# One key load of an attention decode kernel cut by rows: the last sixteen partitions first, in five pieces, then the other 112

## The chip, the cores and the metric

The kernel runs on one core of a Trainium2 chip. The metric is the device time of one execution in microseconds (us). Three runs of the kernel before gave a median of 678.96 us, from 678.95 to 679.36. One further execution was profiled: it took 678.87 us, of which 677.6 us are the span that the profile shows.

## What is computed

One decoded token passes through an attention block and a gated feed-forward block, each behind an adaptive layer norm. The attention reads a key and a value cache of 32 heads, 16384 tokens and 128 numbers per head in bf16: two times 134 MB, which is nearly all that the kernel reads.

```python
mod = (silu(c) @ w_mod).reshape(1, 6, 1, 640)          # sa, ca, ga, sb, cb, gb
h = layernorm(x) * (1 + ca) + sa
q = (h @ wq).reshape(1, 1, 32, 128).transpose(0, 2, 1, 3)
scores = einsum('bhqd,bhkd->bhqk', q, k_cache) * 128 ** -0.5
o = einsum('bhqk,bhkd->bhqd', softmax(scores), v_cache)
x = x + ga * (o.reshape(1, 1, 4096) @ wo)
h = layernorm(x) * (1 + cb) + sb
x = x + gb * ((silu(h @ w_gate) * (h @ w_up)) @ w_down)
```

## The kernel before, in words

The heads are taken in 16 pairs (`NP = 16`). For one pair, the 128 partitions hold two heads by 64 stretches of tokens: partition r holds 256 consecutive tokens (`T2 = 256`) of 128 numbers, which is 65,536 bytes. The keys of a pair are thus one load of 8 MiB with 128 rows of 64 KiB, and so are its values. `k_src(p)` is that view of the key cache. The keys go into `kring`, which has two slots; pair p uses slot `p % 2`. The values go into `vbuf`, which has one slot (the last pair's values go into slot 0 of `kring`).

Per pair, the vector engine (DVE) multiplies the keys by the query in place and folds the 128 products of a token down to 16 columns. This is done in two halves c = 0 and 1: `mult` (L544), `fold` (L549), `foldb` (L554). The tensor engine (PE) adds the 16 columns into the scores (`R`, L534). For pair p-1 the largest score is found and the exponentials are taken while pair p is being multiplied (`largest`, `weigh`), and then PE multiplies them with the values (`pv`, L508). Pairs 0 and 15 go through `score_end` (L562, L568) instead.

All large loads are issued by SyncE (SP) in program order through one helper, `dma` (L90). Each waits on SP for the work that frees its buffer:

- `load_k(p)` for p of 2 and more waits for the last `R` of pair p-2 (`o_R[p - 2]`), which is the last reader of that slot.
- `load_v(p)` waits for `pv` of pair p-1 (`o_pv[p - 1]`).
- The order on SP is: the weights of the modulation and of q, keys 0 (in two halves by tokens, `KCUT`), keys 1, values 0, then in turn keys p+1 and values p, and at the end `wo`, the gate and up weights and five loads of the down weights.

Every load has its own counting semaphore by a key, here `("k", p % 2, c)`, where c numbers the loads of the pair. The first multiplication of pair p waits for `d_k[p][-1]`, the last load of its keys, which in the kernel before is the only one for all pairs from 1 on.

For PE the pairs 1 to 14 are one loop; for DVE and ScalarE the loop begins with pair 3 (`FIRST = 3`), and SP has no loop. Pair 2, the third one, is thus written out on DVE, and its extra waits are plain instructions there.

Of the kernel before, what the change touches and what calls it, by code (L numbers as in the profile page):

```python
# [37 lines left out]
class _Plan:  # L38
# [38 lines left out]
    def op(self, eng, fn, deps=(), name="", chan=None):  # L77
        o = _Op(eng, fn, list(deps), name, len(self.ops), self.loop.get(eng), chan)
        o.sig = chan is not None
        self.ops.append(o)  # L80
        return o

    def dma(self, out_ap, in_ap, key, deps=(), name="", eng="sp", noncontig=False):
        nc = self.nc

        def fn(e, out_ap=out_ap, in_ap=in_ap, noncontig=noncontig):
            if noncontig:
                with nc.allow_non_contiguous_dma(reason="tiny vector layout change"):
                    return e.dma_start(out_ap, in_ap)
            return e.dma_start(out_ap, in_ap)  # L90

        return self.op(eng, fn, deps, name, chan=self.dma_chan(key))
# [116 lines left out]
def build(nc, A_x, A_k, A_v, A_wq, A_wo, B_wg, B_wu, B_wd, c_in, w_mod, out):  # L209
# [6 lines left out]
    T2 = 2 * S // 128  # L216
# [16 lines left out]
    with es:  # L233
        plan = _Plan(nc, es)
        op, dma = plan.op, plan.dma
        POOL, ACT, DVE, PE = "pool", "act", "dve", "pe"

        def sb(name, shape, dtype):
            return es.enter_context(nc.sbuf_tensor(name, list(shape), dtype))

        kring = sb("kring", [128, 2, T2, 128], BF16)
# [27 lines left out]
        rows = qbc[0:1].rearrange("p a d -> p (a d)")[:, 0:2 * D].rearrange("p (j n) -> p j n", j=2)  # L269
# [67 lines left out]
        k_src = lambda p: A_k[0, 2 * p:2 * p + 2].rearrange("h (q t) d -> (h q) t d", q=64)  # L337
# [95 lines left out]
        def pick(half, n, o_m, free):  # L433
# [14 lines left out]
            deps=[o_m0, o_xn], name="t1")  # L448
# [9 lines left out]
        o_qev = []  # L458
        o_q = []
        for g in range(H // 4):  # L460
            b = g % 2
# [9 lines left out]
            for half in range(2):  # L471
# [4 lines left out]
                    deps=[o_q[g]], name="qbc%d_%d" % (g, half)))  # L476
# [4 lines left out]
        d_k, d_v = [None] * NP, [None] * NP  # L481
        o_R, o_pv, o_exp, o_nb, o_mx, o_acc, o_ot = ([None] * NP for _ in range(7))
        KCUT = [0, T2 // 2, T2]
        LCUT = [0, T2 // 2, 7 * T2 // 8, T2]
        VCUT = [0, T2]
        v_at = lambda p: vbuf[:] if p < NP - 1 else kring[:, 0]

        def load_k(p):
            deps = [o_R[p - 2]] if p >= 2 else ([o_mod[1]] if p == 1 else [])
            cuts = KCUT if p == 0 else [0, T2]  # L490
            d_k[p] = [dma(kring[:, p % 2, a:b], k_src(p)[:, a:b], ("k", p % 2, c), deps=deps, name="dma_k%d_%d" % (p, c))
                      for c, (a, b) in enumerate(zip(cuts, cuts[1:]))]

        def load_v(p):
            deps = [o_R[NP - 2]] if p == NP - 1 else [o_pv[p - 1]] if p >= 1 else [o_q[-1]]
# [43 lines left out]
        def score(p, c, between=None):  # L539

            kv4 = kring[:, p % 2].rearrange("p t (a d) -> p t a d", a=2)[:, :, :, QW * c:QW * c + QW]
            def f_mult(e):
                q4 = qbc[:, bass.ds(plan.at(p), 1), :].rearrange("p o (a d) -> p o a d", a=2)[:, :, :, QW * c:QW * c + QW].broadcast_to([128, T2, 2, QW])
                return e.tensor_tensor(out=kv4, in0=kv4, in1=q4, op=ALU.mult)  # L544
            o_m = op(DVE, f_mult,
                     deps=[d_k[p][-1]] + o_qev[p // 2], name="mult%d_%d" % (p, c))
            if between:
                between[0]()
            o_f = op(DVE, lambda e: e.tensor_tensor(out=kv4[:, :, 0], in0=kv4[:, :, 0], in1=kv4[:, :, 1], op=ALU.add),  # L549
                     deps=[o_m], name="fold%d_%d" % (p, c))  # L550
            if between:
                between[1]()
            lo = kv4[:, :, 0]
            return op(DVE, lambda e: e.tensor_tensor(out=lo[:, :, 0:QR], in0=lo[:, :, 0:QR], in1=lo[:, :, QR:QW], op=ALU.add),  # L554
                      deps=[o_f], name="fold%d_%db" % (p, c))

        def score_end(p, c, between=None):

            cut = KCUT if p == 0 else LCUT
            n = cut[c + 1] - cut[c]  # L560
            kv = kring[:, p % 2, cut[c]:cut[c + 1]]
            o = op(DVE, lambda e: e.tensor_tensor(  # L562
                out=kv, in0=kv, in1=qbc[:, p, :].unsqueeze(1).broadcast_to([128, n, 128]), op=ALU.mult),
                deps=[d_k[p][min(c, len(d_k[p]) - 1)]] + o_qev[p // 2], name="mult%d_%d" % (p, c))
            for i, w in enumerate((64, 32, 16)):
                if between and i < 2:
                    between[i]()
                o = op(DVE, lambda e, w=w: e.tensor_tensor(out=kv[:, :, 0:w], in0=kv[:, :, 0:w], in1=kv[:, :, w:2 * w], op=ALU.add),  # L568
                       deps=[o], name="fold%d_%d_%d" % (p, c, w))
            return o  # L570

        def reduce_end(p, a, b, fold):
            def f_R(e):
                last = None
                for d in range(16):
                    last = e.matmul(S_ps[:, a:b], lhsT=ident[:], rhs=kring[:, p % 2, a:b, d], start=(d == 0), stop=(d == 15))  # L576
                return last
            return op(PE, f_R, deps=[fold, o_ident, o_exp[p - 1] if p else o_gb], name="R%d_%d" % (p, a))

        def largest(p):  # L580
            o_pm = op(DVE, lambda e: e.tensor_reduce(  # L581
                out=pm[:, p % 2:p % 2 + 1], in_=S_ps[:, 0:T2], axis=AX.X, op=ALU.max), deps=[o_R[p]], name="pm%d" % p)
            o_d2 = op(ACT, lambda e: e.activation(out=d2[:], in_=negid[:], func=ACTF.Copy, scale=pm[:, p % 2:p % 2 + 1]),  # L583
                      deps=[o_pm, o_negid], name="d2_%d" % p)
            o_mx[p] = op(PE, lambda e: e.matmul(mx_ps[:, 0:64], lhsT=bd_f[:], rhs=d2[:], start=True, stop=True),  # L585
                         deps=[o_d2, o_bd1, o_bd2, o_nb[p - 1] if p >= 1 else o_m0], name="mx%d" % p)
# [14 lines left out]
        def step(p):  # L601
            reduce_mm(p, 0, score(p, 0, before(p)))
            pv(p - 1)
            o_R[p] = reduce_mm(p, 1, score(p, 1))
            diag(p - 1)

        load_k(0)
        load_k(1)
        load_v(0)
        score_end(0, 0)  # L610
        o_R[0] = reduce_end(0, 0, T2, score_end(0, 1))
        NLOOP = NP - 2
        for p in range(1, NP - 1):
            plan.in_loop(("pe",), "pairs", p - 1, NLOOP)
            if p >= FIRST:
                plan.in_loop(("act", "dve"), "pairs", (p - FIRST) // 2, (NP - 1 - FIRST) // 2)
            load_k(p + 1)
            step(p)
            load_v(p)
# [13 lines left out]
        for c in (1, 2):  # L633
            f1 = score_end(PL, c)
            o_R[PL] = reduce_end(PL, LCUT[c], LCUT[c + 1], f1)
        largest(PL)
# [9 lines left out]
        for i, (b, r0, r1) in enumerate(DOWN):  # L646
            if b is None:
                dst, src = wt_v, B_wd[NF * 128:F, :].rearrange("q (h n) -> (q h) n", h=2)
            else:
# [8 lines left out]
                 deps=[o_exp[PL], o_rz, o_onesf, o_rstd], name="L")  # L658
# [7 lines left out]
                  deps=[o_z, o_e32] + o_qev[-2], name="am")  # L666
# [21 lines left out]
        def f_cols(e):  # L688
# [14 lines left out]
            deps=[o_ga, o_xf], name="x1")  # L703
# [18 lines left out]
        def gate0(o_xc1):  # L722
# [6 lines left out]
            deps=[o_xc1, o_rstd1, o_onep_b], name="t2")  # L729
# [6 lines left out]
                  deps=[o_xsp, o_ot[PL], o_strips], name="x1_rows")  # L736
# [10 lines left out]
        for i, (b, r0, r1) in enumerate(DOWN):  # L747
# [14 lines left out]
            if i == 0:  # L762
                o_tw = op(PE, lambda e: e.matmul(attn_ps[:, 8:9], lhsT=twice[64:128].rearrange("p q h -> p (q h)"), rhs=gu_col[64:128, NF:FCH], start=True, stop=True),
                          deps=[o_gum, o_twice, o_abf], name="twice_gu")
                o_guh = op(DVE, lambda e: e.tensor_tensor(out=gu_half[:], in0=attn_ps[:, 8:9].broadcast_to([128, 2]), in1=even[:], op=ALU.mult),
                           deps=[o_tw, o_even], name="gu_half")
# [10 lines left out]
def bass_adaLN_cond__gqa_block_cached__swiglu_ffn__decode_kernel(  # L777
    nc: bass.Bass,
    A_x: bass.AP,
    A_k_cache: bass.AP,  # L780
    A_v_cache: bass.AP,
    A_wq: bass.AP,
    A_wo: bass.AP,
    B_x: bass.AP,
    B_w_gate: bass.AP,
    B_w_up: bass.AP,
    B_w_down: bass.AP,
    c: bass.AP,
    w_mod: bass.AP,
    out: bass.AP,  # L790
):
    build(nc, A_x, A_k_cache, A_v_cache, A_wq, A_wo, B_w_gate, B_w_up, B_w_down, c, w_mod, out)
# [28 lines left out]
```

## Time and profile before

| What | Value |
|---|---|
| Median of 3 runs | 678.96 us (678.95 to 679.36) |
| Profiled execution | 678.87 us, span 677.6 us |
| Bytes read from HBM | 290.47 MB |
| Busy share of the span | DVE 76%, PE 54%, ACT 7% |
| Mean transfer rate | 429 GB/s |
| Loads of keys | 17 issues, 16 pairs |

The span is what the table's shares refer to; the 1.3 us between span and execution lie around it. A busy share is a mean over stages, so the DMA rows by slices and the waits say more than it does about what sets the end. "DMA share" is the mean busy share of the core's 16 DMA engines; "SPq" rows are SP issuing a transfer, not the transfer itself.

### The profile page before, as it was taken

The numbers are of one execution on the slowest core, as the hardware profiler recorded it, in microseconds if no ns is written. First come the engines' busy times: TensorE is split into PE (matmuls) and PEld (weight loads), VectorE is DVE, ScalarE is ACT, GpSimd is POOL, SyncE is SP. The second block draws the span as 40 slices with busy tenths as digits, with TensorE's granted clock in tenths as the row PEclk, the third lists the DMA queues.
The fourth block names the chain that finished last, engine by engine and source line by source line (L and its number), as shares of the span: only waits on it lengthen the run. The fifth ranks groups of instructions, "written<-read, shape, count | busy, mean of one in ns | idle before, by whom it ended". The sixth has DMA issues, their size and how long they took to land.

```text
span 677.6 us, 5406 instructions
## 1 busy us (share of the span) xinstructions
PE 363.6 (54%) x2069; PEld 144.5 (21%) x2069; DVE 514.1 (76%) x190; ACT 46.4 (7%) x146; POOL 0.7 (0%) x6
## 2 busy tenths in 40 slices
PE   2420475755728284654818375562828465481776
PEld 1100122221212122221302122121212222130335
DVE  2189997959596896959597795959699695959912
ACT  1120000100000000000000010000000000000010
POOL 0000000000000000000000000000000000000000
PEclk9675565555757565565756556575656556565765
DMA  9999999999999999999999999999999999999997
GB/s 375 440 459 433 433 437 430 433 430 433 433 434 433 433 433 433 433 433 433 433 433 433 433 433 433 433 433 433 433 433 433 433 433 433 433 433 433 430 400 318
DMA packets 6355, 290.58 MB, mean 429 GB/s; under 512 B 714, under 2 KB 972, under 8 KB 1356
## 3 DMA queue, kind: packets, MB, share of 16 engines
q1 hardware_dynamic: 6340, 290.48, 99.3%
q8 instruction: 5, 0.08, 0.0%
q14 instruction: 2, 0.02, 0.0%
q10 hardware_dynamic: 8, 0.00, 0.0%
HBM read 290.47 MB, written 0.00 MB: 429 GB/s over the span
## 4 chain that ended last, share of the span: by engine, by line
DMA 49%; DVE 30%; issue 13%; PE 8%; SPq 0%; DVEq 0%
DMA kring<-in_A_k_cache_dram 45%; DVE kring L544 10%; PE psb L534 7%; DVE kring L549 6%; DVE kring L562 5%; DVE kring L568 5%; DMA kring<-in_B_w_down_dram 4%; DVE kring L554 3%; SPq L90 0%; DVE pm L581 0%; DVE nb L589 0%; PE psb L576 0%; PE psb L758 0%; DVEq L191 0%; DVEq L544 0%
## 5 line engine op out<-in xcount | busy, mean ns | idle before, releaser
L544 DVE TENSOR_TENSOR kring<-kring,qbc 128x16384 bf16<-128x16384 bf16 x28 | 243.3, 8690 | 96.1 <-DMA kring<-in_A_k_cache_dram 96.1
L534 PE MATMUL psb<-kring,ident 128*128 x448 | 197.5, 607 | 120.3 <-DVE kring L554 120.3
L549 DVE TENSOR_TENSOR kring<-kring 128x8192 bf16<-128x8192 bf16 x28 | 123.8, 4421 | 0.5
L534 PEld LDWEIGHTS psb<-kring,ident 128*128 128x128 bf16 x448 | 54.0, 120 | 248.0 <-issue 247.2
L508 PE MATMUL psb<-vbuf,PZ 128*8 128x512 bf16 x960 | 80.9, 511 | 0.0
L585 PE MATMUL psb<-d,bd_f 128*128 128x64 f32 x32 | 11.0, 446 | 118.5 <-ACT d L583 118.5
L554 DVE TENSOR_TENSOR kring<-kring 128x4096 bf16<-128x4096 bf16 x28 | 64.1, 2288 | 0.5
L562 DVE TENSOR_TENSOR kring<-kring,qbc 128x16384 bf16<-128x16384 bf16 (+2 forms) x5 | 34.9, 6981 | 23.4 <-DMA kring<-in_A_k_cache_dram 23.4
L508 PEld LDWEIGHTS psb<-vbuf,PZ 128*8 128x8 bf16 x960 | 26.6, 108 | 58.9 <-issue 49.0
L576 PE MATMUL psb<-kring,ident 128*128 128x256 bf16 (+3 forms) x64 | 14.5, 392 | 43.2 <-DVE kring L568 43.2
L585 PEld LDWEIGHTS psb<-d,bd_f 128*128 128x128 f32 x32 | 8.0, 312 | 120.7 <-DVE pm L581 111.3
L568 DVE TENSOR_TENSOR kring<-kring 128x2048 bf16<-128x2048 bf16 (+7 forms) x15 | 32.2, 2148 | 0.4
L523 PEld LDWEIGHTS psb<-sel,acc_sb 128*128 128x128 f32 x128 | 28.5, 311 | 7.7 <-issue 4.3
L523 PE MATMUL psb<-sel,acc_sb 128*128 128x2 f32 x128 | 25.6, 322 | 1.1 <-ACT acc_sb L514 1.1
L514 ACT ACTIVATE acc_sb<-psb 128x512 f32<-128x512 f32 x16 | 9.6, 598 | 210.7 <-PE psb L508 210.7
L593 ACT ACTIVATE PZ<-psb,nb 64x256 bf16<-64x256 f32 x32 | 15.0, 469 | 64.8 <-DVE nb L589 64.6
L576 PEld LDWEIGHTS psb<-kring,ident 128*128 128x128 bf16 x64 | 6.4, 121 | 50.5 <-DVE kring L568 44.3
L583 ACT ACTIVATE d<-negid,pm 128x64 f32<-128x64 f32 x16 | 5.6, 348 | 153.2 <-DVE pm L581 153.2
L466 PE MATMUL psb<-vbuf,h_col 128*128 128x512 bf16 x40 | 10.9, 443 | 8.6 <-DMA vbuf<-in_A_wq_dram 8.6
L527 ACT ACTIVATE OT_sb<-psb 128x2 f32 (+1 forms) x16 | 2.8, 172 | 152.2 <-PE psb L523 152.2
L581 DVE TENSOR_REDUCE pm<-psb 128x1 f32<-128x256 f32 x16 | 6.7, 419 | 1.2 <-PE psb L576 1.2
L466 PEld LDWEIGHTS psb<-vbuf,h_col 128*128 128x128 bf16 x40 | 4.1, 112 | 15.3 <-DMA vbuf<-in_A_wq_dram 9.0
(105 smaller groups left out, 79.2 us busy)
## 6 DMA issues: line engine op xcount, KB each, us to landing
kring<-in_A_k_cache_dram SPq DMA_DIRECT2D x2, 4096.0 KB, 40.1
vbuf<-in_A_wq_dram SPq DMA_DIRECT2D x1, 5120.0 KB, 25.8
kring<-in_w_mod_dram SPq DMA_DIRECT2D x1, 4800.0 KB, 14.1
vbuf<-in_A_wo_dram SPq DMA_DIRECT2D x1, 3200.0 KB, 20.6
kring<-in_B_w_gate_dram SPq DMA_DIRECT2D x1, 2160.0 KB, 20.6
kring<-in_B_w_up_dram SPq DMA_DIRECT2D x1, 2160.0 KB, 25.4
vbuf<-in_A_wo_dram SPq DMA_DIRECT2D x1, 1920.0 KB, 24.8
kring<-in_B_w_down_dram SPq DMA_DIRECT2D x3, 640.0 KB, 27.6
```

Of the source, the lines that this page charges most:

```text
L466: last = e.matmul(q_ps[b][:, 0:512], lhsT=h_col[:, k:k + 1].broadcast_to([128, 128]), rhs=wq_v[:, k, g * 512:(g + 1) * 512], start=(k == 0 ...
L508: last = e.matmul(acc_ps[32 * s:32 * s + 8, :], lhsT=PZ[:, j, :], rhs=v_at(p)[:, 4 * j:4 * j + 4, :].rearrange("p t d -> p (t d)"), start= ...
L523: last = e.matmul(OT_ps[:, 0:2], lhsT=acc_sb[:, 128 * i:128 * (i + 1)], rhs=sel[:, i:8:4], start=(i == 0), stop=(i == 3))
L534: last = e.matmul(S_ps[:, 0:T2], lhsT=ident[:], rhs=kring[:, bass.ds(plan.slot(p), 1), :, d].rearrange("p o t -> p (o t)"), start=(d == 0) ...
L544: return e.tensor_tensor(out=kv4, in0=kv4, in1=q4, op=ALU.mult)
L549: o_f = op(DVE, lambda e: e.tensor_tensor(out=kv4[:, :, 0], in0=kv4[:, :, 0], in1=kv4[:, :, 1], op=ALU.add), deps=[o_m], name="fold%d_%d" ...
L554: return op(DVE, lambda e: e.tensor_tensor(out=lo[:, :, 0:QR], in0=lo[:, :, 0:QR], in1=lo[:, :, QR:QW], op=ALU.add), deps=[o_f], name="fol ...
L562: o = op(DVE, lambda e: e.tensor_tensor(out=kv, in0=kv, in1=qbc[:, p, :].unsqueeze(1).broadcast_to([128, n, 128]), op=ALU.mult), deps=[d_k ...
L568: o = op(DVE, lambda e, w=w: e.tensor_tensor(out=kv[:, :, 0:w], in0=kv[:, :, 0:w], in1=kv[:, :, w:2 * w], op=ALU.add), deps=[o], name="fol ...
L576: last = e.matmul(S_ps[:, a:b], lhsT=ident[:], rhs=kring[:, p % 2, a:b, d], start=(d == 0), stop=(d == 15))
L585: o_mx[p] = op(PE, lambda e: e.matmul(mx_ps[:, 0:64], lhsT=bd_f[:], rhs=d2[:], start=True, stop=True), deps=[o_d2, o_bd1, o_bd2, o_nb[p - ...
L593: o_exp[p] = op(ACT, lambda e, half=half, ps=ps: e.activation(out=PZ[ps, :, 4 * half:4 * half + 4], in_=S_ps[ps, 0:T2].rearrange("p (c i) ...
```

## The change

The third pair's keys (p = 2) are no longer one load of 128 rows but six loads, issued one after another on SP:

- rows 112 to 116, 117 to 121, 122 to 126 and 127 alone, each with only the last 16 of the 256 tokens (4 KiB of a row): four loads of 5, 5, 5 and 1 rows;
- rows 112 to 127 with their first 240 tokens (60 KiB of a row): one load of 16 rows;
- rows 0 to 111 whole (64 KiB of a row): one load of 112 rows.

The bytes are the same. The six loads have six semaphores, and the first multiplication of each pair now names all the loads of its keys. All other pairs have their loads as before.

```diff
         KCUT = [0, T2 // 2, T2]
+        UP, UT, UROWS = 2, T2 - 16, [112, 117, 122, 127, 128]
...
         def load_k(p):
             deps = [o_R[p - 2]] if p >= 2 else ([o_mod[1]] if p == 1 else [])
             cuts = KCUT if p == 0 else [0, T2]
-            d_k[p] = [dma(kring[:, p % 2, a:b], k_src(p)[:, a:b], ("k", p % 2, c), deps=deps, name="dma_k%d_%d" % (p, c))
-                      for c, (a, b) in enumerate(zip(cuts, cuts[1:]))]
+            rows = [(0, 128, a, b) for a, b in zip(cuts, cuts[1:])]
+            if p == UP:
+                rows = [(r, s, UT, T2) for r, s in zip(UROWS, UROWS[1:])] + [(112, 128, 0, UT), (0, 112, 0, T2)]
+            d_k[p] = [dma(kring[r:s, p % 2, a:b], k_src(p)[r:s, a:b], ("k", p % 2, c), deps=deps, name="dma_k%d_%d" % (p, c))
+                      for c, (r, s, a, b) in enumerate(rows)]
...
             o_m = op(DVE, f_mult,
-                     deps=[d_k[p][-1]] + o_qev[p // 2], name="mult%d_%d" % (p, c))
+                     deps=(d_k[p] if c == 0 else [d_k[p][-1]]) + o_qev[p // 2], name="mult%d_%d" % (p, c))
```

## Prediction

> **What bounds the kernel now.** I read the page's slices and queues first, to see which resource is never idle.
>
> ```profile
> span 677.6 us, 5406 instructions
> DMA  9999999999999999999999999999999999999997
> GB/s 375 440 459 433 433 437 430 433 430 433 433 434 433 433 433 433 433 433 433 433 433 433 433 433 433 433 433 433 433 433 433 433 433 433 433 433 433 430 400 318
> DMA packets 6355, 290.58 MB, mean 429 GB/s; under 512 B 714, under 2 KB 972, under 8 KB 1356
> q10 hardware_dynamic: 8, 0.00, 0.0%
> DMA 49%; DVE 30%; issue 13%; PE 8%; SPq 0%; DVEq 0%
> ```
>
> The DMA engines are busy in every one of the 40 slices, and the rate stands at 433 GB/s. No other engine looks like that. The chain of work that ended last names DMA for 49% only; that share alone would leave room for another bound, so I looked at two middle periods by windows, and at what the multiplications wait for.
>
> ```profile
> core 0: us, PE busy (x) PEld busy (x) DVE busy (x) ACT busy (x) POOL busy (x), PEclk, DMA share, GB/s
> 221.60:260.30 38.70, 22.03 (x107) 8.06 (x107) 31.01 (x8) 2.24 (x7) 0.00 (x0) 0.54 1.00 434
> 260.30:299.00 38.70, 21.83 (x108) 8.15 (x108) 31.01 (x8) 2.24 (x7) 0.00 (x0) 0.59 1.00 434
> DVE kring L544 <- DMA kring<-in_A_k_cache_dram: 96.1, 13, 8.3
> ```
>
> One pair takes 38.70 us, in which the 16 DMA engines are full (share 1.00) and DVE works 31.01 us. Thirteen times DVE waits for keys, 96.1 us in all, up to 8.3 each. So the transfers set the pace and DVE has some 7.7 us per pair to spare. A delay in the stream of transfers is therefore not made up later: each later pair still needs its 38.70 us of full engines. Now the place of the change, on SP's and DVE's timelines:
>
> ```profile
> 77.28 0.33 SPq L90 DMA_DIRECT2D kring<-in_A_k_cache_dram  x1
> 98.36 0.33 SPq L90 DMA_DIRECT2D vbuf<-in_A_v_cache_dram  x1
> 108.37 0.33 SPq L90 DMA_DIRECT2D kring<-in_A_k_cache_dram  x1
> 105.53 8.69 DVE L544 TENSOR_TENSOR kring<-kring,qbc 128x16384 bf16<-128x16384 bf16 x1 [4.39 <-DMA kring<-in_A_k_cache_dram]
> 144.90 8.69 DVE L544 TENSOR_TENSOR kring<-kring,qbc 128x16384 bf16<-128x16384 bf16 x1 [8.29 <-DMA kring<-in_A_k_cache_dram]
> ```
>
> Keys 2 are issued at 77.28, values 1 at 98.36, keys 3 at 108.37. The first multiplication of pair 2 starts at 105.53 after 4.39 us of waiting for its keys, the one of pair 3 at 144.90 after 8.29. Half a period, 38.70 / 2 = 19.35 us, is one load, so keys 2 move from about 105.5 - 19.35 = 86.2 on, behind values 0. DVE is already waiting for this load, so each microsecond by which it lands later counts in full.
>
> **The change part by part.** *Issue.* One load becomes six. For their price, the last loads of the kernel, and the same rows show what several loads in a row do to the engines:
>
> ```profile
> 644.91 3.16 SPq L90 DMA_DIRECT2D kring<-in_B_w_down_dram  x5
> 670.00:671.00 1.00, 1.00 (x35) 1.00 (x34) 0.00 (x0) 0.00 (x0) 0.00 (x0) 0.50 1.02 415
> 671.00:672.00 1.00, 1.00 (x36) 1.00 (x34) 0.00 (x0) 0.00 (x0) 0.00 (x0) 0.50 1.01 410
> 144.26 0.05 DVEq L191
> ```
>
> Five issues took 3.16 us, 0.63 each, so six take at most 0.33 + 5 x 0.63 = 3.5 us and end near 80.8. The stream reaches them at 86.2, and SP's next issue is at 98.36: hidden, at no cost. Without that cover only the first issue would count, as now. In the end windows short loads follow one another at a DMA share of 1.01 to 1.02 and 410 to 415 GB/s. The 64 KiB of short pieces at that rate instead of 434 lose 0.01 us. Five more waits on DVE at 0.05 us (the wait row at 144.26) are 0.25 us; they are passed while DVE waits for the last load, and queued behind them is only the multiplication that needs the data. I take nothing, at most 0.25.
>
> *Bytes per DMA engine.* The count of small packets tells how a load is spread. SP issues 44 large loads of 128 rows; with 16 completions each they give 704. The two one-row loads of c and x leave one completion each, and the two stores of two rows leave two small data packets and two completions each: 704 + 2 + 8 = 714, the number in the page, and q10's 8 packets fit as well. So a 128-row load is on 16 engines, a one-row load on one, two rows on two. I extend this: 5 rows on five engines, 16 rows on sixteen with one row each, 112 rows on sixteen with seven each. One engine moves 434 / 16 = 27.1 GB/s, a row of 65,536 bytes in 2.42 us and 4 KiB in 0.15 us. If the short loads always fall to the same first engines, engine 0 gets three pieces plus the single row and loses 4 KiB of its long row: +12 KiB, +0.45 us; engines 1 to 4 get +8 KiB, +0.30; the other eleven get -4 KiB, -0.15 us. By bytes per engine alone the change is between -0.15 and +0.45 us.
>
> *Which partitions are written at one time.* This is the disputed term. Before, each of the 16 engines has eight rows of every load, and all 128 partitions are written side by side; the rows above can't say whether 27.1 GB/s belongs to the engine or to the eight partitions at its far end. After, all sixteen engines first write partitions 112 to 127 only. The trace has no load of this shape, so I bound it. If the limit is the engine's alone, the 16 rows pass in one row's time, 2.42 us. If every group of eight partitions has a path of 27.1 GB/s, the 16 rows lie on between two paths (eight rows each, 8 x 2.42 = 19.4 us) and eight (two rows each, 4.8 us). Of 2, 4 and 8 paths I take the middle one, four rows on each of four paths: 4 x 2.42 = 9.7 us. Meanwhile twelve of the sixteen paths carry nothing, and the engines can't run ahead to the next rows since each works its own queue in order.
>
> [...]
>
> The 112 rows would take 7 x 2.42 = 16.9 us if only engines counted. With paths they can't beat a path that still has all of its eight rows, 19.4 us. And an engine's share of seven successive rows straddles groups of eight, so that two engines meet on one path: seven rows, two of them at half rate, are 7 x 2.42 + 2 x 2.42 = 21.8 us. I take 21.8, with 19.4 as the lower end.
>
> *Sum.* Before, the load took 19.4 us. After: 9.7 + 21.8 = 31.5, so +12.1 us; at the ends 4.8 + 19.4 - 19.4 = +4.8 and 19.4 + 19.4 - 19.4 = +19.4. It is put on the stream at the place where DVE waits, with 4.39 us of waiting already there, and nothing after it has idle transfer time to give back. The profiled execution of 678.87 becomes 690.97; the median of the runs is 0.09 us above it, so 691.1. Values 1, keys 3 and all that follow shift by the same amount; what is late next is the same wait, DVE for keys.
>
> **The rivals.**
>
> *The engines alone set the rate* (no change): the price is -0.15 to +0.45 us, hence 678.8 to 679.4. For it: k and v rows run at one flat rate whatever they write. Against: all those rows write 128 partitions. It decides if the 16 rows pass in about 2.4 us. The same comes out if an engine belongs to its partitions: rows 112 to 127 would then fall to the engines that carry them anyway, and each still moves eight rows. [...] Chance 0.17.
>
> *Engines evened out* (faster): the engines don't finish together, and eleven of them are relieved of 4 KiB.
>
> ```profile
> 673.00:673.50 0.50, 0.50 (x19) 0.24 (x15) 0.01 (x1) 0.00 (x0) 0.00 (x0) 0.50 0.86 294
> 673.50:674.00 0.50, 0.50 (x16) 0.28 (x12) 0.15 (x1) 0.00 (x0) 0.00 (x0) 0.50 0.37 138
> 674.00:674.50 0.50, 0.11 (x4) 0.00 (x0) 0.00 (x0) 0.00 (x0) 0.00 (x0) 0.50 0.28 96
> 645.86 28.65 DMA kring<-in_B_w_down_dram
> ```
>
> From 673.0 the engines have 0.5 x (0.86 + 0.37 + 0.28) = 0.76 us of work each left on average, and the last lands at 645.86 + 28.65 = 674.51. Ended evenly, that is 673.8: 0.7 us to gain at most. The change shifts 0.15 of it if the late engines are among the eleven, for 678.8; it decides only if the far ends don't collide. A gain over 0.2% (1.36 us, about what a measurement of this kernel can tell from no change) would need more than the whole unevenness. Chance of that 0.03.
>
> *Rows dealt one by one*: if the 112 rows go to the engines in turn and not in shares of seven, each of the seven rounds writes only 16 neighbouring partitions: 7 x 9.7 = 67.9 us, and +9.7 + 67.9 - 19.4 = +58.2, so 737. Chance 0.07.
>
> *A fixed cost per load in series*: if each short load holds the stream until it has landed, five more loads cost something each. [...] By rows, I bound it by one row's time for the five, 2.42 us: 681.4. Chance 0.07.
>
> **How the numbers follow.** The forecast, colliding writes at +4.8 to +19.4, has 0.66; with the two slower rivals, slower has 0.80, no change 0.17 and faster 0.03. The time is that of the forecast, 691.1. Its own range is 683.7 to 698.4. To leave out no more than 2 in 10 the range must reach down to no change: 678.7 to 698.5, leaving out the faster case and the dealt rows.
>
> **What would show it.** Right: SP has six issues from 77.28 to about 80.8; the first multiplication of pair 2 starts near 117.6 instead of 105.53, with some 16 us of waiting before it; the rate in the slices from 85 to 118 us drops below 433 (12.1 us x 434 GB/s = 5.3 MB missing); afterwards the period is 38.70 again, and everything to the end is late by the same amount. Wrong: if that multiplication starts within 1 us of 105.53, the far ends don't collide and the time is unchanged; if it starts at 160 or later, the rows are dealt one by one; if the lateness shrinks from pair to pair, the stream was not the bound.

## The result and the profile after

The changed kernel takes 701.5 us in the median (700.11 to 702.70, 6 runs) against 679.04 us before on the same chip: the ratio is 1.0329, with a 95% interval of 1.0316 to 1.0342. It is 22.5 us slower. The direction was forecast, the size was not: 691.1 was predicted and the range ended at 698.5.

First the page of the changed kernel, with the slices that answer to those of before (one slice is now 17.5 us).

```profile
span 700.2 us, 5412 instructions
DMA  9999979999999999999999999999999999999997
GB/s 393 427 424 468 363 172 258 382 438 421 431 449 427 427 431 449 431 427 423 449 438 423 427 438 445 427 427 431 449 431 423 434 449 427 427 423 449 438 399 305
```

The rate falls to 172 and 258 GB/s in the sixth and seventh slices, around 88 to 123 us; the slices beside them, with 363 and 382, hold the edges of the same dip. The busy row hardly shows it: it stands at 7 tenths in the sixth slice and at 9 in the seventh, where the rate is down by two fifths. In this kernel the GB/s row tells what the busy row hides.

Then SP's and DVE's timelines and four windows of the changed kernel (in a window the last two columns are the DMA share and the GB/s; a packet, here a row of a load, counts whole where it starts).

```profile
77.16 2.10 SPq L90 DMA_DIRECT2D kring<-in_A_k_cache_dram  x6
100.05 0.35 SPq L90 DMA_DIRECT2D vbuf<-in_A_v_cache_dram  x1
108.24 0.35 SPq L90 DMA_DIRECT2D kring<-in_A_k_cache_dram  x1
128.13 8.69 DVE L548 TENSOR_TENSOR kring<-kring,qbc 128x16384 bf16<-128x16384 bf16 x1 [27.12 <-DMA kring<-in_A_k_cache_dram]
84.00:95.00 11.00, 8.18 (x28) 2.31 (x32) 10.96 (x3) 0.58 (x3) 0.00 (x0) 0.50 0.99 126
95.00:128.00 33.00, 13.56 (x80) 5.33 (x72) 5.98 (x2) 0.77 (x2) 0.00 (x0) 0.55 0.96 254
166.00:204.70 38.70, 21.74 (x106) 7.88 (x106) 31.01 (x8) 2.24 (x7) 0.00 (x0) 0.59 1.00 434
204.70:243.40 38.70, 21.45 (x107) 7.96 (x106) 31.01 (x8) 2.24 (x7) 0.00 (x0) 0.59 1.00 434
```

The six issues take 2.10 us and are over at 79.3, before the stream gets to them. The first multiplication of the third pair starts at 128.13 instead of 105.53, after 27.12 us of waiting for keys: 22.6 us late, which is all of the loss. From there on a period of 38.70 us moves its bytes at 434 GB/s again, and twelve pairs later the lateness is the same. The first multiplication of pair 14, before and after, starts 22.65 us apart:

```profile
570.16 8.69 DVE L544 TENSOR_TENSOR kring<-kring,qbc 128x16384 bf16<-128x16384 bf16 x1 [7.47 <-DMA kring<-in_A_k_cache_dram]
592.81 8.69 DVE L548 TENSOR_TENSOR kring<-kring,qbc 128x16384 bf16<-128x16384 bf16 x1 [7.59 <-DMA kring<-in_A_k_cache_dram]
```

So nothing is lost later and nothing is won back. The two windows at 84 to 95 and 95 to 128 are roughly the two parts of the load: sixteen rows at 126 GB/s, then 112 rows at 254 GB/s. Both rates are somewhat high, because each window also counts the first rows of what follows its part. The engines are held up, and yet they count as busy, with shares of 0.99 and 0.96.

### The profile page after: what moved, and what is told of

Same layout as the page of the kernel before. It is cut to its first block, busy times and chain, and to the rows that moved or that the text cites. A ratio compares the mean times of both kernels' runs of the same rounds, so it can differ in the third digit from the quotient of the medians.

```text
span 700.2 us, 5412 instructions
## 1 busy us (share of the span) xinstructions
PE 361.2 (52%) x2068; PEld 143.9 (21%) x2069; DVE 514.1 (73%) x190; ACT 46.4 (7%) x146; POOL 0.7 (0%) x6
## 4 chain that ended last, share of the span: by engine, by line
DMA 49%; DVE 29%; issue 12%; PE 7%; another core or an unknown queue 1%; SPq 1%; DVEq 0%
DMA kring<-in_A_k_cache_dram 45%; DVE kring L548 10%; DVE kring L553 6%; PE psb L538 6%; DVE kring L566 5%; DVE kring L572 5%; DMA kring<-in_B_w_down_dram 4%; DVE kring L558 2%; PE psb L580 1%; SPq L90 1%; DVE pm L585 0%; DVE nb L593 0%; PE psb L762 0%; DVEq L191 0%
## 5 line engine op out<-in xcount | busy, mean ns | idle before, releaser
L512 PE MATMUL psb<-vbuf,PZ 128*8 128x512 bf16 x960 | 78.1, 497 | 0.8 <-DMA vbuf<-in_A_v_cache_dram 0.8
L512 PE MATMUL psb<-kring,PZ 128*8 128x512 bf16 x64 | 6.4, 590 | 1.9 <-DMA kring<-in_A_v_cache_dram 1.9
```

The costliest lines, as they stand in the source:

```text
L512: last = e.matmul(acc_ps[32 * s:32 * s + 8, :], lhsT=PZ[:, j, :], rhs=v_at(p)[:, 4 * j:4 * j + 4, :].rearrange("p t d -> p (t d)"), start= ...
```

## The experiments

All of them change only the loads of the third pair's keys. One leaves sixteen rows out, and two put the rows into other partitions than their values have; these three show times only, since their third pair is not the attention that was asked for. The theories were:

- **A, the far end:** the time is set by which partitions the sixteen engines write at one moment.
- **B, the source:** it is set by which rows of the cache they read at one moment.
- **C, the number of loads:** each further load costs a fixed time.

In the diffs a row of the list is (rows, tokens) or, where `slice` stands, (target rows, source rows, tokens).

**Eight loads that all span 128 partitions.**

```diff
-                rows = [(r, s, UT, T2) for r, s in zip(UROWS, UROWS[1:])] + [(112, 128, 0, UT), (0, 112, 0, T2)]
+                rows = [(0, 128, 32 * c, 32 * c + 32) for c in range(8)]
```

> The third pair's keys come in eight loads cut by tokens (32 tokens each), every one over all 128 partitions. Theory A (far end: the time is set by which partitions the sixteen engines write at the same time): nothing changes beside short rows, 679.0 to 679.6. Rival B (source: the time is set by which rows of the cache are read together): 679.0 as well, the rows read together are those of before. Rival C (number of loads: each further load costs a fixed time in series): the changed kernel has five loads more and is 22.5 us slower, 4.5 us each; seven more give +31, 710.

Measured: 679.66 us against 679.33, ratio 1.0005 (0.9996 to 1.0015). Seven more loads than before cost nothing that this measurement can tell from zero (by the interval at most 1.0 us), where rival C needed 31 us. C falls.

**Source against target.** Four kernels, each with eight loads of 16 rows. In two of them the target rows are neighbours (by blocks) and in two they lie eight apart (by strides); likewise the source rows.

```diff
+  by blocks:                 (slice(16 * c, 16 * c + 16), slice(16 * c, 16 * c + 16), 0, T2) for c in range(8)
+  by strides:                (slice(c, 128, 8), slice(c, 128, 8), 0, T2) for c in range(8)
+  blocks read, strides written:  (slice(c, 128, 8), slice(16 * c, 16 * c + 16), 0, T2) for c in range(8)
+  strides read, blocks written:  (slice(16 * c, 16 * c + 16), slice(c, 128, 8), 0, T2) for c in range(8)
```

By blocks:

> The third pair's keys come in eight loads of 16 neighbouring rows each (0-15, 16-31, ...). Theory A: each load is like the sixteen rows of the changed kernel, four engines on one path: 8 x 4 x 2.42 = 77 us at least instead of 19.4, +58; with the 10.3 us that a row of 60 KiB took there, 8 x 11.0 = 88, +69. So 737 to 748. Rival B: the same, since the rows read together are neighbours too. Rival C: seven more loads, +31, 710.

By strides:

> The third pair's keys come in eight loads of 16 rows that lie eight apart (0, 8, 16, ... 120, then 1, 9, ... and so on). Theory A, if the paths belong to eight neighbouring partitions: every engine has its own path, 679 to 680. Theory A, if they are mixed over the partitions: between that and four engines on one path, +58. [...] Rival B: the rows read together lie 512 KiB apart in the cache; no row here gives a price, between 679 and 748. Rival C: +31, 710.

Blocks read, strides written:

> Eight loads of 16 rows: each reads 16 neighbouring rows of the cache (as in the loads by blocks) and writes them to partitions eight apart (as in the loads by strides). The keys of the third pair thus stand in other partitions than its values. Theory A (far end): the time of the loads by strides, within 1 us. Rival B (source): the time of the loads by blocks, within 1 us. Rival C: 710.

Strides read, blocks written:

> Eight loads of 16 rows: each reads rows eight apart in the cache and writes 16 neighbouring partitions, the mirror of the run that read neighbours and wrote strides. The keys of the third pair thus stand in other partitions than its values. Theory A (far end): the time of the loads by blocks, +55.5, 735, within 1.5 us. Rival B (source): the time of the loads by strides, 702.

| read \ written | 16 neighbours | 16 rows eight apart |
|---|---|---|
| 16 neighbours | 734.8 us (+55.5) | 702.84 us (+23.5) |
| 16 rows eight apart | 734.81 us (+55.5) | 702.14 us (+22.8) |

The time follows the column. By blocks it came out 2 us below the expected 737 to 748. By strides it is neither of the two ends that were named: had each group of eight neighbouring partitions a path of its own, as the prediction supposed, no time would have been lost. One window from the middle of the load in each of the four, in the table's order by rows:

```profile
90.00:150.00 60.00, 16.41 (x96) 6.19 (x94) 11.08 (x3) 0.77 (x2) 0.00 (x0) 0.56 1.04 123
90.00:120.00 30.00, 16.66 (x96) 6.23 (x94) 11.03 (x3) 0.77 (x2) 0.00 (x0) 0.61 1.01 208
90.00:150.00 60.00, 16.37 (x96) 6.16 (x94) 11.09 (x3) 0.77 (x2) 0.00 (x0) 0.56 1.03 122
90.00:120.00 30.00, 17.74 (x96) 6.43 (x94) 10.89 (x3) 0.77 (x2) 0.00 (x0) 0.56 1.00 206
```

Sixteen neighbouring partitions take 122 to 123 GB/s whatever is read, sixteen that lie eight apart take 206 to 208, and the DMA share is full in all four. A window counts whole packets, so its edges blur the rate; by the total times the 8 MiB took 19.4 + 55.5 = 74.9 us by blocks (112 GB/s) and 19.4 + 22.8 = 42.2 us by strides (199 GB/s). If a path carries 434 / 16 = 27.1 GB/s, as the prediction supposed, that is, as an estimate, the rate of about 4.1 and of 7.3 paths. B falls; A stands.

**Where the 22.5 us lie.** One kernel drops the four short pieces; another leaves the sixteen rows out altogether.

```diff
+  two whole loads:    rows = [(112, 128, 0, T2), (0, 112, 0, T2)]
+  rows 0-111 alone:   rows = [(0, 112, 0, T2)]
```

> Two loads only: rows 112-127 whole, then rows 0-111 whole; the four short pieces are gone. Theory A (the time is set by which partitions the sixteen engines write together): the same as the changed kernel, +22.5, 701 to 702. Rival C (short pieces and number of loads cost): most of the 22.5 goes; eight loads by tokens cost 0.3 us, so this rival is left with the pieces being on few engines, 0.45 us.

> Rows 0-111 of the third pair's keys alone; rows 112-127 are left out (the partitions keep old data). The load moves 7/8 of the bytes. If engines alone counted: 16.9 instead of 19.4 us, -2.4, 676.6. The prediction's term: 21.8 us, +2.4, 681.4. If the sixteen rows cost 10 of the changed kernel's 41.9 us and this load the other 32: +12, 691. Nothing waited for out of turn may blur this by a microsecond.

Two whole loads: 701.31 us (700.43 to 702.19), +22.0 over its 679.33, like the changed kernel; the four short pieces cost nothing that shows. Rows 0-111 alone: 691.88 us (691.70 to 692.05), +12.6. So the load of 112 rows, with an eighth less to move, takes 12.6 + 19.4 = 32.0 us (229 GB/s) instead of the 21.8 that the prediction gave it. The other sixteen rows are 701.31 - 691.88 = 9.4 us, where it had 9.7; with two runs of each, this difference is good to about 1 us.

**Why 112 rows take 32 us.** Seven loads of sixteen rows seven apart write, one after the other, the seven sets of rows that a load of 112 writes if engine e works off rows 7e to 7e + 6 in order.

```diff
+                rows = [(slice(112, 128), slice(112, 128), 0, T2)] + [(slice(c, 112, 7), slice(c, 112, 7), 0, T2) for c in range(7)]
```

> Rows 112-127 whole, and rows 0-111 in seven loads of 16 rows seven apart (0, 7, ... 105, then 1, 8, ... 106, and so on). If a load of 112 rows gives each engine seven successive rows, worked off in order, these seven loads write the same partitions in the same seven rounds: the time of the two whole loads, 701 to 702, within 1 us. If the 112 rows are given to the engines in another order, the time differs: between 689 (no collisions in the seven loads, 10 + 19.4 - 19.4) and 737 (four engines on one path in each).

Measured: 702.81 us (702.15 to 703.47). That is 1.5 us above the 701.31 of the two whole loads, a little more than the 1 us expected, though the two ranges touch. Since another order could lie anywhere between 689 and 737, the time alone does not settle it, and the course of the rounds has to. The windows of its seven rounds, and below them the rounds of the kernel with rows 0-111 alone (its first window holds the end of the load before):

```profile
95.60:100.40 4.80, 4.41 (x60) 1.49 (x52) 4.76 (x2) 0.34 (x1) 0.00 (x0) 0.76 0.97 218
100.40:105.10 4.70, 3.83 (x9) 1.11 (x10) 0.72 (x1) 0.26 (x1) 0.00 (x0) 0.97 1.03 223
105.10:110.00 4.90, 4.72 (x16) 2.64 (x14) 0.00 (x0) 0.14 (x1) 0.00 (x0) 0.50 0.67 217
110.00:112.60 2.60, 0.00 (x0) 0.00 (x0) 0.00 (x0) 0.03 (x1) 0.00 (x0) 0.50 1.15 328
112.60:116.20 3.60, 0.00 (x0) 0.00 (x0) 0.00 (x0) 0.00 (x0) 0.00 (x0) 0.50 1.11 273
116.20:121.00 4.80, 0.00 (x0) 0.00 (x0) 0.00 (x0) 0.00 (x0) 0.00 (x0) 0.50 1.00 218
121.00:125.60 4.60, 0.00 (x0) 0.00 (x0) 0.00 (x0) 0.00 (x0) 0.00 (x0) 0.50 0.97 228
```

```profile
84.00:88.50 4.50, 2.38 (x6) 0.82 (x7) 4.50 (x2) 0.62 (x3) 0.00 (x0) 0.50 1.15 262
88.50:93.20 4.70, 4.70 (x15) 1.21 (x17) 4.70 (x1) 0.00 (x0) 0.00 (x0) 0.50 1.02 223
93.20:97.90 4.70, 4.70 (x64) 1.49 (x56) 4.67 (x2) 0.00 (x0) 0.00 (x0) 0.75 0.95 223
97.90:101.00 3.10, 0.02 (x4) 0.00 (x0) 3.07 (x2) 0.60 (x1) 0.00 (x0) 1.00 0.85 275
101.00:104.50 3.50, 3.31 (x8) 1.04 (x9) 0.05 (x1) 0.00 (x0) 0.00 (x0) 0.70 1.03 300
104.50:109.00 4.50, 4.50 (x15) 2.11 (x13) 0.00 (x0) 0.00 (x0) 0.00 (x0) 0.50 1.10 248
109.00:113.70 4.70, 0.75 (x4) 0.66 (x4) 0.00 (x0) 0.17 (x1) 0.00 (x0) 0.50 1.01 227
```

Both have the same course: three rounds near 220 GB/s, two faster ones, two near 220 to 250 (the 262 at the top of the second list holds the end of the load before). So the 112 rows have the course that shares of seven successive rows have, and in the seven loads five of the seven rounds run at about half of 434 GB/s (217 to 228) for all sixteen engines together: 4.6 to 4.9 us per round instead of 2.42.

The packet records of the trace, which have every row's own time, show who is slow. Before, a row of 64 KiB took 2.42 us. In the changed kernel sixteen rows are under way at a time, and between 84 and 131 us each row starts within 0.1 us of the end of another, as if each engine took its rows one after the other. Of the changed kernel, the sixteen rows that start between 102.2 and 105.4 us, a slow round, took 4.46 to 4.98 us each. Of the sixteen that start between 107.2 and 109.8 us, the first of the two faster rounds, two took 4.50 and 4.55 us, and the other fourteen 2.58 to 3.56. Of the sixteen of the second faster round, between 110.8 and 113.5 us, one took 4.29 us and the other fifteen 2.75 to 3.43. So in the faster rounds one or two rows take nearly twice their time while the others do much better; in the slow round all sixteen do.

That all of them slow down was not expected. Why they do is not shown by any run here. Nor does a run with rows seven apart separate the rows read from the rows written, as the four kernels above did for blocks and strides of eight.

**Row sets that cost nothing, and one that does.**

```diff
+  every second row:  (slice(c, 128, 2), slice(c, 128, 2), 0, T2) for c in range(2)
+  every fourth row:  (slice(c, 128, 4), slice(c, 128, 4), 0, T2) for c in range(4)
+  halves:            (0, 64, 0, T2), (64, 128, 0, T2)
```

> Two loads of 64 rows two apart (even rows, then odd rows). Together each load writes partitions all over the 128. Theory A by rounds (what counts is which sixteen partitions are written at one moment, four successive even rows per engine being worked off in order): in each round the sixteen rows lie eight apart, as in the loads by strides of eight, so the same +22.8, 702. Theory A by span (what counts is whether the load as a whole reaches all partitions groups): 679 to 680.

> Four loads of 32 rows four apart (0, 4, ... 124, then 1, 5, ... 125, and so on). If 32 rows are dealt like the 64 rows two apart, so that each engine stays on its own path: no change, 679 to 680. If an engine gets two successive rows and works them off in order, as with the 112 rows, each round writes sixteen rows eight apart, as in the loads by strides of eight: +22.8, 702.

> Two loads of 64 neighbouring rows: 0-63, then 64-127. The loads of every second row (also 64 rows) cost nothing, so 64 rows are not given to the engines as four successive rows each, worked off in order. Theory A1 (the engine goes with the partition that it writes: eight engines carry rows 0-63 and the other eight go on to rows 64-127): no change, 679 to 680. Theory A2 (all sixteen engines share 64 rows, whichever they are, and 64 neighbouring rows have half of the paths): each row at half rate, two loads of 4 x 5.1 = 20.4 us and more instead of one of 19.4, +19 to +23, 698 to 702.

Every second row: 679.25 us, ratio 1.0000 (0.9988 to 1.0011). Every fourth row: 679.21, ratio 0.9999 (0.9988 to 1.0009). Halves: 702.07, +22.8. A window inside the load of each, in that order:

```profile
87.00:104.00 17.00, 13.90 (x85) 4.08 (x84) 14.23 (x3) 0.60 (x1) 0.00 (x0) 0.70 1.01 436
87.00:104.00 17.00, 14.31 (x86) 4.17 (x85) 13.91 (x3) 0.60 (x1) 0.00 (x0) 0.70 1.00 432
88.00:120.00 32.00, 19.52 (x101) 6.96 (x99) 13.07 (x3) 0.77 (x2) 0.00 (x0) 0.55 1.08 222
```

For every second and every fourth row the one alternative, that an engine gets successive rows of its load and works them off in order, falls: that order would have written rows eight apart together, at 206 GB/s. These loads run at the full rate (436 and 432 GB/s), so here no two engines hold each other up; that each stays on a path of its own is the plain reading of it, but it is not shown, since no trace names the engine of a row. The halves come out at the upper end of the range of theory A2, 702.07 of 698 to 702, with 222 GB/s inside the load, about half of the full rate; the half of the paths in A2 is an assumption of the author's.

**The same shift of bytes, written widely.** The short pieces stay; only 4 KiB of each of rows 0-111 go in a load of 112 rows, and the rest in one load of 128.

```diff
+                rows = [(r, s, UT, T2) for r, s in zip(UROWS, UROWS[1:])] + [(0, 112, UT, T2), (0, 128, 0, UT)]
```

> The same bytes on the same engines as in the changed kernel, but with little of it written narrowly: the four short loads as they are, rows 0-111 with their last 16 tokens in one load, then all 128 rows with their first 240 tokens in one load. Theory A: the 112-row load took 32.0 us for 64 KiB a row, so 2.0 us for 4 KiB instead of 1.06; the sixteen short rows take 4 x 0.15 = 0.6 instead of 0.15; +1.4 in all at most, 680.0 to 680.7. If relieving eleven engines of 4 KiB is worth anything, it is 0.15 us less. Rival C: +0.3 as for eight loads by tokens, 679.6.

Measured: 680.88 us against 679.31, ratio 1.0022 (1.0013 to 1.0032), +1.6, a little above the "at most" +1.4. With a sixteenth of the bytes on narrow sets of rows the loss is a fourteenth of the 22.5 us, and nothing of the relief of eleven engines by 4 KiB shows. No version here is faster than the kernel before.

## Why the prediction was right or wrong

The place and the kind of the loss were right: what counts is which partitions are written together (+55.5 us for sixteen neighbours and about +23 for sixteen that lie eight apart, whatever was read). The transfers set the pace, the third pair's first multiplication waits for the slower load (until 128.13 us, where 117.6 was forecast), the lateness passes one to one to the end, and the period after it is unchanged at 38.70 us. SP's issues are hidden, as said, though they take 2.10 us rather than 3.5.

The step that failed is the size of the load of 112 rows. Its term was 7 x 2.42 + 2 x 2.42 = 21.8 us; it measured 32.0. The working let only the two engines that meet on a path run at half rate, for two of seven rows. The seven rounds show instead that in five of them all sixteen engines slow to about half (217 to 228 GB/s of 434); something like the assumed picture, two rows at 4.50 and 4.55 us and the others better off at 2.58 to 3.56, is found only in the first of the other two, and in the second with one slow row. The groups behind this working were wrong as well: it gave every eight neighbouring partitions one path, and by that sixteen rows eight apart would have cost nothing, where they cost 22.8 us. The upper end of the range was no help, since it doubled the sixteen rows' term and left this one at 19.4; with the forecast's own 21.8 in its place it would have reached 700.8, still short of 701.5.

The other large term held: 9.7 us for the sixteen rows, four on each of four paths, against 9.4 measured by difference. There was luck in this: four was taken only as the middle of 2, 4 and 8 paths, and no row of the profile before spoke for it. Nor does it go with the groups of the other term, since sixteen neighbouring rows lie in two groups of eight. The sum was thus 9.7 + 21.8 - 19.4 = +12.1 where 9.4 + 32.0 - 19.4 = +22.0 would have been right, the figure of the two whole loads. The small terms, pieces on few engines (up to 0.45 us) and five more waits on DVE (up to 0.25), don't show.

Of the rivals, engines alone (no change) is refuted by the blocks and strides, and the fixed cost per load by the eight loads by tokens. Rows dealt one by one would have given 737; the 112 rows have the course of the seven loads of rows seven apart instead, which is that of shares in order. Evening out the engines is left unproved: in the changed kernel the loss covers it, and in the last experiment it does not show either.

## What to carry to other kernels

Where transfers set the pace, cut a load along its free dimension (eight loads by tokens took 679.66 us against 679.33), or take rows evenly spread over all 128 partitions in large enough numbers (every second or fourth row cost nothing, every eighth cost 22.8 us); loads of some neighbouring rows lost time here (55.5 us with sixteen rows in each, 22.8 with 64, and 12.6 for the 112 rows alone, with an eighth less to move), and the loss stayed to the end (22.65 us at pair 14 of the changed kernel). To move a few KiB between engines, count what every other row of that load then costs. Watch the rate and not the busy share: here the DMA engines were "busy" at 0.99 with 126 GB/s.

## What the runs showed that was not expected

- In five of the seven rounds of the 112 rows all sixteen engines slow to about half (217 to 228 GB/s of 434 in the seven loads of rows seven apart; 4.46 to 4.98 us for a row in a slow round of the changed kernel, instead of 2.42), and not only two of them, as in the prediction's working. In the two faster rounds two rows and then one take 4.29 to 4.55 us, and the others do better with 2.58 to 3.56. The reason is open.
- How rows are given to engines seems to depend on the load: 112 rows have the course of successive rows in order, but 64 and 32 evenly spread rows keep the full rate (436 and 432 GB/s), which shares of successive rows would not: they would write rows eight apart together, and those ran at 206.
